# A retention-attention and MLP kernel: attention in pairs of units grouped by array tiling, far parts a period later, row factors in the masks

## The chip, the cores and the metric

The kernel runs on one core of a Trainium2 chip. The metric is the device time of one execution in microseconds. Before the change the median of 3 runs is 662.73 (660.90 to 663.81).

## What is computed

Batch 4, 8 heads, 576 positions, 64 columns per head, all in fp32 inputs. Attention without a softmax, with a decay per head, and then two MLP blocks:

```python
scores = scale * np.matmul(q, k.transpose(0, 1, 3, 2))
gamma = 1.0 - 2.0 ** (-5.0 - np.arange(H, dtype=np.float32))
Dmat = np.where(rel >= 0, gamma[:, None, None] ** rel[None, :, :], 0.0)
ret = scores * Dmat[None, :, :, :]
return np.matmul(ret, v)
...
h = gelu(x @ w_in)
u, v = (h[..., :d_ff // 2], h[..., d_ff // 2:])
v_s = np.einsum('ts,bsd->btd', w_sg, layer_norm(v) * g_ln) + b_sg[None, :, None]
x = x + (u * v_s) @ w_out
...
x = x + np.maximum((layer_norm(x) * g_ln2) @ w_ch1, 0.0) @ w_ch2
```

## The kernel before

The change lies in the first of three stages, the attention. Its work is 16 units: a unit is one batch and one pair of heads, whose 2x64 columns lie on the two halves of the 128 partitions. A sequence of 576 is four chunks of 128 and a rest of 64. Since the decay is a power of the distance, a unit needs only four products on TensorE (PE). A pair of units here is an even unit and the odd one after it; the rests of both are done together.

- `scores(n)` (L246): k times q of each chunk, two heads, into two PSUM banks. The scores are multiplied by a triangular mask with the factors of the key's row (L256): three of four masks of a pair on VectorE (DVE), the fourth copied by ScalarE (ACT, L254) and multiplied by GpSimd (POOL). For odd units also the rest scores of both units (L269, masked by L273).
- `states(n)` (L282): k, scaled by ACT beforehand (L237 in `prep_unit`), times v, per chunk; a scan on DVE (L290) adds them up with the decay into y.
- `attend_near(n)` (L315): masked scores times v.
- `attend(n)` (L327): the far part, y of the chunk before times q, added in the same bank; DVE multiplies the result by the row factors of the query (L333) on its way to SBUF. Odd units add the rest: `attend_rest` (L303, v times masked rest scores), L346 (y times q) and DVE's L350.

The array is used in parts. Scores multiply 64 rows into 128 outputs, states and near parts 128 rows into 64 outputs, far and rest parts 64 rows into 64 outputs; the two heads use two parts of the array. Each fp32 product counts as two records in the trace, so that a unit's 8 score instructions are 16 records.

The order of every engine's work is written out by hand (`manual_schedule`): instructions stand on each engine in the order of the program text, and semaphores are put where data need them. The loop over the units does at step n: the load of unit n+3 (one DMA on SP's queue, 1120 KB in a ring of five tiles), `prep_unit(n+2)`, `scores(n+1)`, a number of background steps, then the rest, `states(n+1)`, `attend_near(n)` and `attend(n)`, and more background steps. The first product of the MLP, `v_products(0, 0)`, is placed inside the last unit.

The background (`background_steps`) is a generator. It decodes weights that come as 64-bit words into fp32 and splits each into a high and a low part. A piece of 512 columns is one DMA of 512 KB (`f64_words`, L147) and four DVE instructions (L156, L160, L163, L165), one Square on ACT (L162), then a cast on ACT (L360) and a subtraction on POOL (L361), spread over four steps: w_in first (8 pieces), then w_sg (5 loads of fp32, split without a decode), then w_out and pieces of w_ch, which go back to DRAM. `UNIT` gives the number of steps at the two places of each unit; the last `LATE` pieces of w_ch are decoded in the MLP.

Before the loop, DVE forms the masks from a table (L499, L507), ACT forms the scan's decay (L524), PE makes `WARM` products of zeros (L530, two passes each) and `form_rows` makes the query's row factors with four products and an ACT copy (L515, L519). DVE, ACT, POOL and SP stand beside PE; there are eight PSUM banks, one of them for the decode.

Of the kernel before, what the change touches and what calls it, by code (L numbers as in the profile page):

```python
# [21 lines left out]
NP = H // 2  # L22
# [14 lines left out]
WARM = 3  # L37
# [9 lines left out]
LATE = 5  # L47
UNIT = "00 00 21 22 31 11 10 12 21 13 22 11 32 20 01 32".split()
# [26 lines left out]
O_MASKR = 16  # L75
O_HEAD = O_MASKR + NP * R
O_GROW = O_HEAD + C
TA = O_GROW + NP * C
TS = (NP + 1) * C
# [8 lines left out]
def const_tables():  # L88
    g = np.array(GAMMA, np.float64)
    p = np.arange(128)  # L90
    tab = np.zeros((128, TF + TS), np.float64)
# [3 lines left out]
    for hp in range(NP):  # L95
        gp = g[2 * hp + p // D][:, None]
        tab[:, O_GC + hp * NC:O_GC + (hp + 1) * NC] = gp ** C * (np.arange(NC)[None, :] > 0)
        tab[:, O_GR + hp:O_GR + hp + 1] = gp ** -(p % R)[:, None]
        tab[0:H, TF + (hp + 1) * C:TF + (hp + 2) * C] = np.arange(H)[:, None] == 2 * hp + p[None, :] // D
    tab[0:H, TF:TF + C] = g[:, None] ** np.arange(C)[None, :] / np.sqrt(D)  # L100
    return tab.astype(np.float32)
# [3 lines left out]
def kernel(  # L105
# [7 lines left out]
    tab_in: bass.AP,  # L113
    params: bass.AP,
# [74 lines left out]
    ld = es_a.enter_context(tc.tile_pool(name="ld", bufs=5))  # L189
# [8 lines left out]
    first = pa.tile([128, D * NC], F32, tag="y", bufs=3, name="first")  # L198

    def load_tab(part):  # L200
        if part == 0:
            nc.sync.dma_start(out=first[:, 0:TF], in_=tab_in[:, 0:TF])
        else:
            nc.sync.dma_start(out=tab[0:H, O_HEAD:], in_=tab_in[0:H, TF:])

    NU = B * NP
    units = {}
# [3 lines left out]
    def load_unit(n):  # L211
        t = ld.tile([128, AW], F32, tag="ld", name="ld")
        if n == 0:

            to, src = (z[:, 0:2 * S].rearrange("p (a s) -> p a s", a=2) for z in (t, attn[n]))
            for x, y in ((0, 2 * C), (2 * C, S)):
                nc.sync.dma_start(out=to[:, :, x:y], in_=src[:, :, x:y])
                if x == 0:
                    load_tab(0)
            nc.sync.dma_start(out=t[:, 2 * S:], in_=attn[n, :, 2 * S:])  # L220
        else:
            nc.sync.dma_start(out=t, in_=attn[n])
        units[n] = dict(ld=t)

    def prep_unit(n):
        u = units[n]
        hp = n % NP
        t = u["ld"]
        u["qT"] = t[:, 0:S]
        u["kT"] = t[:, S:2 * S]  # L230
        u["k"] = t[:, 2 * S:2 * S + NC * C].rearrange("p (c e) -> p c e", c=NC)
        o = 2 * S + NC * C
        v = t[:, o:]
        u["v"] = v
        for h in range(2):
            k = u["k"][:, :, h * D:(h + 1) * D]
            act.activation(out=k, in_=k, func=ACTF.Copy, scale=col(tab, 2 * hp + h))  # L237

    def scores(n):
        u = units[n]  # L240
        hp = n % NP
        p = u["p"] = pa.tile([128, 2, NC, C], F32, tag="p", name="p")
        sc = [bank() for h in range(2)]
        for c in range(NC):
            for h in range(2):
                pe.matmul(  # L246
                    sc[h][:, c * C:(c + 1) * C], u["kT"][h * D:(h + 1) * D, c * C:(c + 1) * C],
                    u["qT"][h * D:(h + 1) * D, c * C:(c + 1) * C], start=True, stop=True,
                )
        for h in range(2):  # L250
            x = sc[h].rearrange("p (c i) -> p c i", c=NC)
            on = dve
# [6 lines left out]
            free(sc[h])  # L259
        if n % 2 == 0:  # L260
            return

        rest = u["rest"] = bank()
        pr = u["pr"] = pa.tile([128, 2 * R], F32, tag="pr", name="pr")
        for x in range(2):
            w = units[n - 1 + x]
            for h in range(2):
                r = slice(h * D, (h + 1) * D)
                pe.matmul(  # L269
                    rest[r, x * R:(x + 1) * R], w["kT"][r, NC * C:], w["qT"][r, NC * C:], start=True, stop=True,  # L270
                    skip_group_check=True,
                )
        dve.tensor_tensor(out=pr, in0=rest[:, 0:2 * R], in1=col(tab, O_MASKR + (hp - 1) * R, 2 * R), op=ALU.mult)  # L273

    def states(n):
        u = units[n]
        us = bank()
        us_c = us[:, 0:NC * D].rearrange("p (e c) -> p c e", c=NC)
        for c in range(NC):
            for h in range(2):  # L280
                r = slice(h * D, (h + 1) * D)
                pe.matmul(  # L282
                    us_c[r, c], u["k"][:, c, r],
                    u["v"][:, c * C + h * D:c * C + (h + 1) * D], start=True, stop=True,
                )


        y = pa.tile([128, D * NC], F32, tag="y", bufs=3, name="y")
        u["y"] = y.rearrange("p (e c) -> p c e", c=NC)
        dve.tensor_tensor_scan(  # L290
# [1203 lines left out]
```

## Time and profile before

| | us |
|---|---|
| median of 3 runs | 662.73 |
| profiled execution | 661.1 |
| its span, first to last instruction | 659.3 |
| PE busy | 652.3 (99%) |
| DVE busy | 458.7 (70%) |
| ACT busy | 310.7 (47%) |
| POOL busy | 306.0 (46%) |
| second `v_products` starts on PE, after the attention | 78.45 |

Times inside the kernel count from the first instruction. The attention stage lies between 7.34 us, the first scores, and 78.45. A busy PE is not a PE at its peak, since matmuls are pipelined and a record overlaps the next one; so lengths are read from start to start. Waits are named by the engine that waits, then the one that ended the wait.

### The profile page before, as it was taken

How to read it: one execution, taken by the hardware profiler on the slowest of the kernel's cores; microseconds unless marked ns; L12 is line 12 of the kernel's file. 1: busy time of each engine (PE TensorE's matmuls, PEld its weight loads, DVE VectorE, ACT ScalarE, POOL GpSimd, SP SyncE). 2: the span in 40 equal slices, each digit the busy share in tenths (PEclk: the TensorE clock that was granted, in tenths of full speed). 3: DMA queues.
4: the chain of work that ended last, by engine and by line, in shares of the span. 5: the costliest groups of instructions: out<-in, count | busy, mean ns of one | idle time of the engine just before them, and what ended most of it. 6: DMA issues, size and time to landing. Idle time of an engine off the chain costs nothing.

```text
span 659.3 us, 12482 instructions
## 1 busy us (share of the span) xinstructions
PE 652.3 (99%) x4428; PEld 592.9 (90%) x4428; DVE 458.7 (70%) x925; ACT 310.7 (47%) x638; POOL 306.0 (46%) x290
## 2 busy tenths in 40 slices
PE   8999999999999999999999999999999999999997
PEld 6888899899889989998898889988898889999996
DVE  5799769789799885877888643555543345458894
ACT  4454595275277457524454533233535313335443
POOL 0354658225325617955555694265558742410000
PEclk9999999999999999999999999999999999999999
DMA  8999638677687685579996868799999689999734
GB/s 317 365 371 352 192 106 231 228 243 231 225 296 230 194 244 135 173 276 398 310 309 245 266 209 269 241 369 371 341 354 373 200 299 342 363 364 413 263 129 160
DMA packets 97230, 181.23 MB, mean 275 GB/s; under 512 B 9608, under 2 KB 47112, under 8 KB 93456
## 3 DMA queue, kind: packets, MB, share of 16 engines
q1 hardware_dynamic: 97168, 180.44, 80.7%
q8 instruction: 35, 0.57, 0.3%
q14 instruction: 27, 0.22, 0.1%
HBM read 122.99 MB, written 56.62 MB: 272 GB/s over the span
## 4 chain that ended last, share of the span: by engine, by line
PE 92%; DVE 3%; DMA 2%; ACT 2%; POOL 1%; issue 1%; SPq 0%; DVEq 0%; POOLq 0%; ACTq 0%
PE b L139 24%; PE b L137 23%; PE b L138 23%; PE b L788 6%; PE b L1265 3%; PE b L246 2%; PE b L315 2%; PE b L327 2%; PE b L1266 2%; DMA raw<-in_w_in_dram 1%; PE b L282 1%; PE b L530 1%; PE b L722 1%; PE b L721 1%; POOL vnl L645 1%
## 5 line engine op out<-in xcount | busy, mean ns | idle before, releaser
L137 PE MATMUL b<-fe,w 128*128 128x384 f32 x336 | 113.2, 337 | 0.0
L139 PE MATMUL b<-fe,w 128*128 128x384 f32 x336 | 113.0, 336 | 0.0
L138 PE MATMUL b<-fe,w 128*128 128x384 f32 x336 | 112.7, 335 | 0.0
L139 PE MATMUL b<-w,h 128*128 128x512 f32 (+1 forms) x270 | 98.1, 363 | 0.0
L138 PE MATMUL b<-w,h 128*128 128x512 f32 (+1 forms) x270 | 97.9, 363 | 0.0
L137 PE MATMUL b<-w,h 128*128 128x512 f32 (+1 forms) x270 | 96.8, 358 | 0.0
L869 POOL TENSOR_TENSOR w<-raw_w,w 128x512 fp32r<-128x512 f32 x30 | 39.6, 1321 | 58.3 <-ACT w L868 53.2
L137 PEld LDWEIGHTS b<-fe,w 128*128 128x128 f32 x336 | 63.1, 188 | 3.8 <-DVE t L1122 0.9
L138 PEld LDWEIGHTS b<-fe,w 128*128 128x128 f32 x336 | 63.1, 188 | 2.7
L139 PEld LDWEIGHTS b<-fe,w 128*128 128x128 f32 x336 | 63.0, 188 | 0.0
L139 PEld LDWEIGHTS b<-w,h 128*128 128x128 f32 x270 | 51.0, 189 | 7.7
L137 PEld LDWEIGHTS b<-w,h 128*128 128x128 f32 x270 | 51.0, 189 | 6.0 <-issue 0.2
L138 PEld LDWEIGHTS b<-w,h 128*128 128x128 f32 x270 | 50.9, 189 | 6.1
L162 ACT ACTIVATE raw<-raw 128x512 f32<-128x512 f32 x44 | 29.9, 679 | 54.5 <-DVE b L160 47.3
L1099 ACT ACTIVATE h<-b 128x384 fp32r<-128x384 f32 x32 | 15.7, 491 | 82.7 <-DVE b L1128 54.7
L589 POOL TENSOR_TENSOR st<-st,par 128x1 f32<-128x1 f32 x36 | 22.1, 616 | 49.6 <-DVE st L588 49.5
L1100 DVE SCALAR_TENSOR_TENSOR h<-b,h 128x384 fp32r<-128x384 f32 x32 | 17.8, 556 | 30.7 <-ACT h L1099 30.7
L137 PE MATMUL b<-w_sg,vnh 128*128 128x288 f32 x128 | 37.8, 295 | 0.0
L139 PE MATMUL b<-xt_hi,w_in 128*128 128x288 f32 x128 | 37.7, 295 | 0.0
L139 PE MATMUL b<-w_sg,vnl 128*128 128x288 f32 x128 | 37.7, 295 | 0.0
L138 PE MATMUL b<-w_sg,vnh 128*128 128x288 f32 x128 | 37.7, 295 | 0.0
L138 PE MATMUL b<-xt_lo,w_in 128*128 128x288 f32 x128 | 37.7, 294 | 0.0
(196 smaller groups left out, 1695.3 us busy)
## 6 DMA issues: line engine op xcount, KB each, us to landing
w<-ws_dram SPq DMA_DIRECT2D x96, 256.0 KB, 5.0
ld<-in_attn_dram SPq DMA_DIRECT2D x15, 1120.0 KB, 8.4
raw<-in_w_ch_dram SPq DMA_DIRECT2D x32, 512.0 KB, 4.9
ws_dram<-w SPq DMA_DIRECT2D x16, 896.0 KB, 7.6
w<-wb_dram SPq DMA_DIRECT2D x14, 1024.0 KB, 7.9
w_dram<-c SPq DMA_DIRECT2D x32, 256.0 KB, 3.1
wb_dram<-fe SPq DMA_DIRECT2D x32, 256.0 KB, 5.1
raw_w<-w_dram SPq DMA_DIRECT2D x30, 256.0 KB, 4.3
```

The costliest lines, as they stand in the source:

```text
L137: pe.matmul(ps, lh, rh, start=first, stop=False, skip_group_check=True)
L138: pe.matmul(ps, lh, rl, start=False, stop=False, skip_group_check=True)
L139: pe.matmul(ps, ll, rh, start=False, stop=last, skip_group_check=True)
L162: act.activation(out=f(w1), in_=f(w1), func=ACTF.Square)
L246: pe.matmul(sc[h][:, c * C:(c + 1) * C], u["kT"][h * D:(h + 1) * D, c * C:(c + 1) * C], u["qT"][h * D:(h + 1) * D, c * C:(c + 1) * C], sta ...
L315: pe.matmul(o[r, c * C:(c + 1) * C], v[:, c * C + h * D:c * C + (h + 1) * D], p[:, h, c], start=(c == 0), stop=(c == NC - 1), skip_group_c ...
L589: pool.tensor_tensor(out=st[:, 4:5], in0=st[:, 3:4], in1=col(par, O_MH), op=ALU.pow)
L788: pe.matmul(ps, g, wo[k][:, w], start=done[0] == 1, stop=done[0] == 3 * KE, skip_group_check=True)
L869: pool.tensor_tensor(out=t[:, 1], in0=raw, in1=f(t[:, 0]), op=ALU.subtract)
L1099: act.activation(out=t[:, 0], in_=v, func=ACTF.Relu)
L1100: dve.scalar_tensor_tensor(out=t[:, 1], in0=v, scalar=0.0, in1=f(t[:, 0]), op0=ALU.max, op1=ALU.subtract)
L1265: pe.matmul(ps, e[:, 0, x], t, start=begin, stop=False, skip_group_check=True)
```

## The change

The loop runs over eight pairs. In one step it does the scores and masks of both units, then the rest scores, then `finish` of the pair before (both far parts, both rest parts, and the copies to SBUF, now on ACT), then the states of both, the scans, and the near parts of both. Pairs 0 and 1 have orders of their own. A unit comes by two DMAs, kT and k in one tile (ring of 4), qT, v and the rest's v in another (ring of 6). Four units are loaded at the start, two more at the end of each step. The row factors of the query are folded into the masks (for the near part) and are multiplied onto q by POOL (for the far part), so that the results are copied without a factor. To form them, a row of 1024 numbers is spread over the partitions by products with a row of ones. w_in is loaded with the second half of its columns first. The pace of the background is now a number of steps per pair (`PAIR`), `LATE` is 6 and `WARM` is 2, and `v_products(0, 0)` follows the last `finish`.

```diff
-WARM = 3
+WARM = 2
-LATE = 5
-UNIT = "00 00 21 22 31 11 10 12 21 13 22 11 32 20 01 32".split()
+LATE = 6
+PAIR = "03 22 22 22 22 23 33 54".split()
...
     def load_unit(n):
-        t = ld.tile([128, AW], F32, tag="ld", name="ld")
+        kk = ld.tile([128, S + NC * C], F32, tag="kk", bufs=4, name="kk")
+        qv = ld.tile([128, S + NC * C + D], F32, tag="qv", bufs=6, name="qv")
...
-            nc.sync.dma_start(out=t, in_=attn[n])
+            nc.sync.dma_start(out=kk, in_=attn[n, :, 0:w])
+            nc.sync.dma_start(out=qv, in_=attn[n, :, w:])
...
+    def scale_q(n):
+        q = units[n]["qT"]
+        row = col(tab, O_LATE + n % NP * C, C)
+        x = q[:, 0:NC * C].rearrange("p (c i) -> p c i", c=NC)
+        pool.tensor_tensor(out=x, in0=x, in1=row.unsqueeze(1).to_broadcast([128, NC, C]), op=ALU.mult)
+        x = q[:, NC * C:]
+        pool.tensor_tensor(out=x, in0=x, in1=row[:, 0:R], op=ALU.mult)
...
-            if h and n % 2:
-                act.copy(p[:, h], x)
-                x, on = p[:, h], pool
-            on.tensor_tensor(
-                out=p[:, h], in0=x, in1=mask[:, 2 * hp + h].unsqueeze(1).to_broadcast([128, NC, C]), op=ALU.mult,
+            dve.tensor_tensor(
+                out=p[:, h], in0=u["sc"][h].rearrange("p (c i) -> p c i", c=NC),
+                in1=mask[:, 2 * (n % NP) + h].unsqueeze(1).to_broadcast([128, NC, C]), op=ALU.mult,
...
-        dve.tensor_tensor(
-            out=xb[b][:, hp, 0:NC * C].rearrange("p (c i) -> p c i", c=NC),
-            in0=o.rearrange("p (c i) -> p c i", c=NC),
-            in1=col(tab, O_GROW + hp * C, C).unsqueeze(1).to_broadcast([128, NC, C]), op=ALU.mult,
-        )
+        act.copy(xb[b][:, hp, 0:NC * C], u["o"])
...
+    each = [bank() for _ in range(2)]
+    for x in range(2):
+        pe.matmul(each[x], one[0:1, 0:128], grow[0:1, x * 512:(x + 1) * 512], start=True, stop=True)
...
+    def form_masks(x):
+        for h in range(x * 4, x * 4 + 4):
+            dve.scalar_tensor_tensor(
+                out=mask[:, h], in0=each[x][:, h % 4 * C:(h % 4 + 1) * C], scalar=col(first, O_GP + h),
+                in1=col(first, O_TRI, C), op0=ALU.mult, op1=ALU.mult,
+            )
...
+    def form_rows():
+        late = bank()
+        for h in range(2):
+            pe.matmul(
+                late[half[h]], one[0:1, 0:D], grow[0:1].rearrange("p (a h i) -> p a h i", h=2, i=C)[:, :, h],
+                start=True, stop=True, skip_group_check=True,
+            )
+        act.copy(col(tab, O_LATE, NP * C), late)
...
+    def finish(k):
+        for n in (2 * k, 2 * k + 1):
+            far(n)
+            put(n)
+        attend_rest(k)
+        put_rest(k)
+
+    for k in range(NPAIR):
+        a, b = 2 * k, 2 * k + 1
+        if k == 0:
+            form_masks(0)
+            scores(a)
+            form_rows()
+            masks(a)
+            scale_k(a)
+            form_masks(1)
+            form_rest()
+            states(a)
+            near(a)
+            background(1)
+            scores(b)
+            scores_rest(k)
+            masks(b)
+            scale_k(b)
+        else:
+            scores(a)
+            masks(a)
+            scale_k(a)
+            if k == 1:
+                finish(k - 1)
+            scores(b)
+            masks(b)
+            scale_k(b)
+            scores_rest(k)
+        mask_rest(k)
+        scale_q(a)
+        scale_q(b)
+        background(int(PAIR[k][0]))
+        if k > 1:
+            finish(k - 1)
+        if k:
+            states(a)
+        states(b)
+        scans(k)
+        if k:
+            near(a)
+        near(b)
+        load_unit(a + 4)
+        load_unit(b + 4)
+        background(int(PAIR[k][1]))
...
+    finish(NPAIR - 1)
```

**Where instructions moved.** PE in one pair of units before. b_76 and the like are PSUM banks; ld is a unit's loaded tile; x8 after a row is a number of equal instructions; of the eight score rows of a unit one or two stand here.

```order
L246 MATMUL b_82<-ld 128x128
L269 MATMUL b_76<-ld 64x64 x4
L282 MATMUL b_77<-ld 64x64 x8
L315 MATMUL b_78<-p,ld 64x128 x8
L327 MATMUL b_78<-ld,y 64x128 x6
L246 MATMUL b_81<-ld 128x128
...
L303 MATMUL b_76<-pr,ld 64x64 x4
L282 MATMUL b_80<-ld 64x64 x8
L315 MATMUL b_82<-p,ld 64x128 x8
L327 MATMUL b_82<-ld,y 64x128 x6
L346 MATMUL b_76<-ld,y 64x64 x4
```

PE after, from the states of pair 1 to the near parts of pair 2:

```order
L285 MATMUL b_77<-qv,kk 64x64 x16
...
L245 MATMUL b_82<-qv,kk 128x128
L245 MATMUL b_77<-qv,kk 128x128
L264 MATMUL b_79<-qv,kk 64x64 x4
L316 MATMUL b_76<-qv,y 64x128 x6
L316 MATMUL b_80<-qv,y 64x128 x6
L331 MATMUL b_78<-pr,qv 64x64 x4
L331 MATMUL b_78<-qv,y 64x64 x4
L285 MATMUL b_81<-qv,kk 64x64 x16
L307 MATMUL b_82<-p,qv 64x128 x8
L307 MATMUL b_77<-p,qv 64x128 x8
```

Groups of one kind of both units now stand together, and the far parts (L316) are those of the pair before. The scores of unit 5 use the bank b_77 in which the states of pair 1 were.

DVE after, from the last decode step of the first w_in piece (L163) to the first mask of unit 4 (L154 is the first decode step of the next piece, L295 the scans of pair 1):

```order
L163 SCALAR_TENSOR_TENSOR c<-raw,b_75 128x512 [waits DVE_49,Activation_49]
L154 TENSOR_SCALAR b_75<-raw 128x512 [waits DMAHW1_49,DVE_49]
L295 SCALAR_TENSOR_TENSOR y<-formed,b_77 128x256 [waits PE_49]
L295 SCALAR_TENSOR_TENSOR y<-formed,b_77 128x256
L158 SCALAR_TENSOR_TENSOR b_75<-raw,b_75 128x512 [waits DVE_49]
L161 SCALAR_TENSOR_TENSOR b_75<-raw,b_75 128x512 [waits DVE_49]
L251 TENSOR_TENSOR p<-b_79,formed 128x512 [waits PE_49,Activation_49]
```

Both scans of one pair and all four masks of the next now stand behind a step that waits for a load; before, one scan and the masks of one unit stood there.

ACT in the opening before (L519 is the copy of the row factors, L237 the scaling of k):

```order
L524 COPY formed<-first 128x256 x4
L237 ACTIVATE ld<-ld,tab 128x4x64 [waits DMAHW3_49,Activation_49]
L237 ACTIVATE ld<-ld,tab 128x4x64
L519 COPY tab<-b_79 128x512 [waits DMAHW4_49,PE_49]
L237 ACTIVATE ld<-ld,tab 128x4x64 [waits DMAHW5_49]
```

and after (L520 and L227):

```order
L500 COPY formed<-first 128x256 x4
L520 COPY tab<-b_81 128x512 [waits PE_49]
L227 ACTIVATE kk<-kk,tab 128x4x64 [waits DMAHW4_49,Activation_49]
L227 ACTIVATE kk<-kk,tab 128x4x64
L227 ACTIVATE kk<-kk,tab 128x4x64 [waits DMAHW6_49]
```

The copy, which waits for PE, has moved ahead of the scaling of unit 0's k.

## Rows read from the trace of the kernel before

**Rows 1.** The page, engines and costliest groups: busy us (share) xinstructions; busy, mean ns | idle

```profile
PE 652.3 (99%) x4428; PEld 592.9 (90%) x4428; DVE 458.7 (70%) x925; ACT 310.7 (47%) x638; POOL 306.0 (46%) x290
...
L869 POOL TENSOR_TENSOR w<-raw_w,w 128x512 fp32r<-128x512 f32 x30 | 39.6, 1321 | 58.3 <-ACT w L868 53.2
```

**Rows 2.** Stretches: length, busy us of PE PEld DVE ACT POOL, clock, DMA share, GB/s

```profile
20.00:60.00 40.00, 39.83 (x701) 35.22 (x696) 37.97 (x69) 21.49 (x44) 20.13 (x16) 1.00 0.97 362
30.00:40.00 10.00, 9.82 (x164) 8.52 (x164) 9.93 (x19) 6.23 (x13) 4.26 (x4) 1.00 1.01 402
60.00:70.00 10.00, 9.96 (x166) 8.64 (x164) 9.31 (x18) 5.91 (x11) 5.36 (x5) 1.00 0.74 274
90.00:100.00 10.00, 10.00 (x78) 10.00 (x77) 6.86 (x23) 9.81 (x22) 6.05 (x7) 1.00 0.29 79
```

**Rows 3.** PE's timeline over one pair: start us, us, engine, line, output, xrecords

```profile
43.82 1.16 PE L246 MATMUL b<-ld 64*128 64x128 f32 x16
44.91 0.45 PE L269 MATMUL b<-ld 64*64 64x64 f32 x8
45.29 0.69 PE L282 MATMUL b<-ld 128*64 128x64 f32 x16
45.81 1.05 PE L315 MATMUL b<-p,ld 128*64 128x128 f32 x16
46.78 0.98 PE L327 MATMUL b<-ld,y 64*64 64x128 f32 x12
47.70 1.16 PE L246 MATMUL b<-ld 64*128 64x128 f32 x16
...
50.66 0.98 PE L327 MATMUL b<-ld,y 64*64 64x128 f32 x12
51.48 0.59 PE L346 MATMUL b<-ld,y 64*64 64x64 f32 x8
52.00 0.38 PE L246 MATMUL b<-ld 64*128 64x128 f32 x2
```

**Rows 4.** PE's timeline, the opening

```profile
2.27 5.14 PE L530 MATMUL b<-zero 128*128 128x512 f32 x6 [2.27 <-ACT zero L495]
7.34 1.16 PE L246 MATMUL b<-ld 64*128 64x128 f32 x16
...
17.24 0.99 PE L327 MATMUL b<-ld,y 64*64 64x128 f32 x12
```

**Rows 5.** PE's timeline, the end of the stage

```profile
72.76 0.50 PE L137 MATMUL b<-w_in,xt_hi 128*128 128x512 f32 x1
...
75.71 0.45 PE L303 MATMUL b<-pr,ld 64*64 64x64 f32 x8
...
78.45 0.50 PE L137 MATMUL b<-w_in,xt_hi 128*128 128x512 f32 x1
```

**Rows 6.** ACT's timeline, the opening

```profile
7.70 0.91 ACT L237 ACTIVATE ld<-ld,tab 128x256 f32<-128x256 f32 x2 [2.46 <-DMA ld<-in_attn_dram]
9.62 0.59 ACT L519 COPY tab<-b 128x512 f32<-128x512 f32 x1 [1.02 <-PE b L515]
```

**Rows 7.** DVE's timeline around its wait for the second w_in piece

```profile
27.13 0.69 DVE L156 TENSOR_SCALAR b<-raw 128x512 uint32<-128x512 uint32 x1 [1.47 <-DMA raw<-in_w_in_dram]
27.73 0.68 DVE L290 TENSOR_TENSOR_SCAN y<-formed,b 128x256 f32<-128x256 f32 x1
...
28.91 0.28 DVE L350 TENSOR_TENSOR xb<-b,tab 128x128 f32<-128x128 f32 x1
29.11 0.69 DVE L160 SCALAR_TENSOR_TENSOR b<-raw,b 128x512 uint32<-128x512 uint32 x1
```

**Rows 8.** DMA issues from 4.7 to 5.0 us: KB each, us to landing

```profile
raw<-in_w_in_dram SPq DMA_DIRECT2D x1, 512.0 KB, 13.5
```

**Rows 9.** ACT's timeline, after the stage

```profile
79.21 1.28 ACT L619 ACT_TABLE_LOAD   x1
```

More of the change, by code (lines that the diff above doesn't have):

```diff
@@ L196 @@
     decay = formed[:, H * C:].rearrange("p (x n) -> p x n", x=NP)
[L198 to L204, printed above, removed]
+    first = pa.tile([128, D * NC], F32, tag="y", bufs=4, name="first")
     NU = B * NP
+    NPAIR = NU // 2
     units = {}
@@ new lines, with scores_rest, mask_rest @@
+    rests = {}
+    def scores_rest(k):
+        t = rests[k] = bank()
+        for x in range(2):
+            u = units[2 * k + x]
+            for r in half:
+                pe.matmul(
+                    t[r, x * R:(x + 1) * R], u["kT"][r, NC * C:], u["qT"][r, NC * C:], start=True, stop=True,
+                    skip_group_check=True,
+                )
+    def mask_rest(k):
+        pr = units[2 * k]["pr"] = pa.tile([128, 2 * R], F32, tag="pr", name="pr")
+        dve.tensor_tensor(
+            out=pr, in0=rests[k][:, 0:2 * R], in1=col(tab, O_MASKR + 2 * k % NP * R, 2 * R), op=ALU.mult
+        )
@@ L244, in scores, with states @@
+    sums = {}
+    def states(n):
+        k, x = divmod(n, 2)
+        if x == 0:
+            sums[k] = bank()
+        u = units[n]
+        o = sums[k][:, x * NC * D:(x + 1) * NC * D].rearrange("p (e c) -> p c e", c=NC)
         for c in range(NC):
@@ L275, in states @@
[L275 to L290, printed above, removed]
-            out=y, data0=decay[:, n % NP], data1=us[:, 0:NC * D], initial=0.0, op0=ALU.mult, op1=ALU.add
-        )
-        free(us)
@@ new lines, in states, with scans @@
+                    start=True, stop=True, skip_group_check=True,
+                )
+    def scans(k):
+        us = sums.pop(k)
+        for x in range(2):
+            y = pa.tile([128, D * NC], F32, tag="y", bufs=4, name="y")
+            units[2 * k + x]["y"] = y.rearrange("p (e c) -> p c e", c=NC)
+            dve.tensor_tensor_scan(
+                out=y, data0=decay[:, (2 * k + x) % NP], data1=us[:, x * NC * D:(x + 1) * NC * D], initial=0.0,
+                op0=ALU.mult, op1=ALU.add,
+            )
+        free(us)
@@ new lines, in attend_rest @@
+    def attend_rest(k):
+        for part in range(2):
+            for x in range(2):
+                u = units[2 * k + x]
+                for r in half:
+                    o = rests[k][r, (2 + x) * R:(3 + x) * R]
+                    if part == 0:
+                        w, z = u["v"][r, NC * C:], units[2 * k]["pr"][r, x * R:(x + 1) * R]
+                    else:
+                        w, z = u["y"][r, NC - 1], u["qT"][r, NC * C:]
+                    pe.matmul(o, w, z, start=part == x == 0, stop=part == 1, skip_group_check=True)
@@ L354, in attend, with put_rest @@
-        free(rest)
+        act.copy(xb[b][:, hp, 0:NC * C], u["o"])
+        free(u["o"])
+    def put_rest(k):
+        b, hp = divmod(2 * k, NP)
+        t = rests.pop(k)
+        act.copy(xb[b][:, hp:hp + 2, NC * C:], t[:, 2 * R:4 * R].rearrange("p (x i) -> p x i", x=2))
+        free(t)
+        for x in range(2):
+            del units[2 * k + x]
     wi, wsl, wo = [], [], []
@@ new lines, in form_rows, with form_rest @@
+    def form_rows():
+        late = bank()
+        for h in range(2):
+            pe.matmul(
+                late[half[h]], one[0:1, 0:D], grow[0:1].rearrange("p (a h i) -> p a h i", h=2, i=C)[:, :, h],
+                start=True, stop=True, skip_group_check=True,
+            )
+        act.copy(col(tab, O_LATE, NP * C), late)
+        free(late)
+    def form_rest():
+        for hp in range(NP):
+            for x in range(2):
+                r = half[x]
+                dve.scalar_tensor_tensor(
+                    out=tab[r, O_MASKR + hp * R:O_MASKR + (hp + 1) * R],
+                    in0=tab[r, O_LATE + hp * C:O_LATE + hp * C + R], scalar=first[r, O_GR + hp:O_GR + hp + 1],
+                    in1=first[r, O_TRI + x * R:O_TRI + (x + 1) * R], op0=ALU.mult, op1=ALU.mult,
+                )
```

230 lines of the change are left out of this document (71 added, 159 removed).

## The prediction, made before the changed kernel ran

> **What bounds the kernel now.** I read the page's engine lines first. PE is busy for 99% of the span and DVE for 70% [rows 1], so the end is set by PE's row of work, and an edit counts only where it shortens that row or makes PE wait. The change touches the first 78 us. There the stretches [rows 2] show what stands close behind PE: from 30 to 40 us DVE is busy for 9.93 of 10 us, and over 20 to 60 us the DMA engines are busy for 0.97 of the time at 362 GB/s. From 90 to 100 us ACT is busy for 9.81 of 10. Then I read PE's timeline over one pair of units [rows 3]: it runs from 43.82 to 52.00, 8.18 us, group after group without a wait. The opening [rows 4] and the end of the stage [rows 5] come last.
>
> **What a change of group costs PE.** Of one unit, the states (L282, 8 steps of 64 columns) take 45.81-45.29 = 0.52 us and the near part (L315, 8 steps of 128) takes 46.78-45.81 = 0.97 [rows 3]. The difference, 0.45, is 8x64 columns: 0.056 us per 64, 0.112 per 128 columns. (Two records that start together, on two parts of the array, are one step.) So pure streaming is 0.90 for the scores of a unit, 0.45 states, 0.90 near, 0.675 far (6x0.112), and 0.225 for each of three rest groups of a pair: 2x2.925+0.675 = 6.525 us. The pair takes 8.18, so 1.65 lies at the group boundaries. Read per group: scores 1.09-0.90 = 0.19, states with near 1.49-1.35 = 0.14, a lone rest group 0.38-0.225 = 0.155, a lone far group 0.92-0.675 = 0.245, and far with the L346 rest 52.00-50.66 = 1.34 against 0.90, so 0.44.
>
> **Pair by pair after the change.** A steady pair is three blocks: scores of both units 16x0.112+0.19 = 1.98; one block of the 64x64 groups (rest scores, both far parts, both rest parts), 12x0.112+12x0.056 = 2.02, with the largest boundary cost of such a block, 0.44, 2.46; states and near parts of both 2.70+0.14 = 2.84. Sum **7.3**, 0.88 less than 8.18. If each of the three boundaries costs the mean of before (1.65/8 = 0.2), it is 7.15; if nothing is saved it is 8.18. Pair 1 has its far block between the two scores: 1.09+2.24+1.09+0.38+2.84 = 7.65. The last far block, alone, is 1.35+0.45+0.44 = 2.24, and the first v product, moved behind it, takes 75.71-72.76 = 2.95 in both kernels [rows 5].
>
> **The opening gets longer.** Before, far(1) starts at 17.24 [rows 4]; by then PE has also done scores(2), states(2), far(0) and the rest group L303 (1.09+0.52+0.92+0.38), so what the new order does up to near(1) is worth 14.33. After: six warm passes take 5.14 us, 0.857 each [rows 4]; now there are four, and four passes of the two one-row products that spread the row factors. Steady 512 columns take 4x0.112 = 0.45. If six passes run at 0.857 and two at 0.45, the first score starts at 8.3 instead of 7.34. The ends are 7.4 (one-row passes at half price) and 9.1 (all at 0.857). Scores end at 9.4, the second row product (4 passes, two side by side, 0.9) at 10.3. On ACT the copy of that product now stands ahead of the two k scalings of unit 0, which before were done at 7.70 to 8.61, ahead of the copy [rows 6]: 0.1+0.55+0.91 makes states(0) start at 11.85, a wait of 1.5. Near(0) ends 13.3, scores(1) 14.4, rest scores 14.8, states(1) 15.3; near(1) needs two masks of 0.60 each on DVE [rows 7] behind scores(1), so it starts at about 15.8 and ends at **16.85**. That is 2.5 more than 14.33.
>
> **Plain sum.** 16.85+7.65+6x7.3+2.24+2.95 = 73.5, where before PE starts the second v product at 78.45 [rows 5]: -4.95.
>
> **Waits that the new order adds.** DVE runs in order, and a decode step of the background stands ahead of scans and masks. (i) The first w_in piece comes behind four units in both kernels; it was issued at about 4.9 and took 13.5 us [rows 8], so it lands at 18.4. Two DVE steps (1.2) and the Square on ACT (0.6) follow, 20.2, then scale_k(2) 0.91, the puts of pair 0 (1.2, as ACT's 128x512 copy), scale_k(3) 0.91: 23.2. PE is at states(3) at 16.85+1.09+2.24+1.09+0.38+0.45 = 22.1: +1.1, less what the masks' own order gives back, 1.0. (ii) The second piece follows two more units (1,146,880 bytes each) and its own 524,288 at 402 GB/s [rows 2]: 18.4+2x2.85+1.3 = 25.4. The first decode step (L154) waits for it ahead of the two scans of pair 1, and those free the bank into which scores(5) write: 25.4+0.6+1.2 = 27.2, while PE is there at 16.85+7.65+1.0+1.0 = 26.5. Take 1.0; ends 0 and 2.5 (the piece as late as before, where L156 waited 1.47 and started at 27.13 [rows 7]). (iii) In pairs 6 and 7 the background runs six and nine steps, and the last w_in piece comes behind units 14 and 15. The nearest row is the same wait of 1.47: take 1.5, ends 0 and 3.0. (iv) 0.3 for short waits of near parts. Together **+3.8**, and the stage ends at 77.3, 1.1 earlier.
>
> **Work moved between engines.** The row factors go into the masks and q: 16 row multiplies and 8 small ones leave DVE (0.60 and 0.20 each by its neighbours [rows 7]), four masks a pair run on DVE instead of three, and ACT copies the results out instead of copying scores. DVE's pair is then, with four decode steps, 4x0.60+0.20+2x0.60+4x0.60 = 6.2, under 7.3; with six it is 7.4. POOL multiplies q once per unit; a 128x512 operation there takes about 1.3 us by the L869 row (39.6 us for 30 [rows 1]), and a pair of 7.3 us holds two of them and its one or two other operations; far, the first reader of the chunks, comes a period later. The two DMAs per unit instead of one add 8x2 issues on SP and no bytes. Because v_products moves behind the last far block, PE has no filler there, and the last puts on ACT stand behind three w_sg copies that wait for loads.
> The Trainium skill, page "TensorEngine Tiling (Array Packing)", Performance Considerations, PSUM Bottleneck, says that packing the array speeds up TensorE but not the emptying of PSUM, which may become the bound. By that rule the gain of 0.88 a pair would not all be kept; the full DVE in the stretch from 30 to 40 us agrees with it, the sum of 6.2 does not.
>
> **Behind the stage.** Before, the table load at 79.21 [rows 9] precedes the first gelu, and ACT is then full until 100 us [rows 2], so a later first gelu reaches PE. The puts behind the w_sg copies, the sixth late w_ch piece (one more decode, 4 steps of 0.60 on DVE and one Square on ACT inside the first MLP block) and the short cover there I price at **+1.5**; ends 0 (all hidden) and 3.0 (two ACT waits like the 1.47).
>
> **Sum:** -1.1+1.5 = +0.4 against the profiled execution's 661.1 (span 659.3), whose time is 1.6 below the median of the runs, 662.73. On the median: **663.1 us**, no change. What a measurement can tell from no change here is about 0.5%, 3.3 us.
>
> **Rivals.** *A, the waits stay hidden (faster).* If pieces land a little sooner and ACT's chain has slack, neither the 3.8 nor the 1.5 reaches PE: -4.95, **657.8**. For it: PE waits almost nowhere before although DVE is full. Against: the order puts L154 straight ahead of scans and masks.
> *B, the transfers become the bound (slower).* A steady pair needs 2x1.147+0.524 = 2.82 MB. At 402 GB/s [rows 2] that is 7.0 us, hidden; at the 362 of 20 to 60 us it is 7.8, 0.5 over 7.3. It decides below 385 GB/s. Six pairs: +3.0 on the forecast, **666.1**. For: share 0.97. Against: 60 to 70 us is at 274 GB/s, so loads run ahead.
> The Trainium skill, page "DMA: Bandwidth & Descriptors", overview table, gives about 358 GB/s from HBM per core; estimated from it, a pair's transfers take 7.9 us and the result is 3.6 above the forecast. The stretch of 402 GB/s disagrees with it as a ceiling.
> *C, the boundary cost is not what grouping removes (slower).* If PE pays per step and not per change of tile form, pairs stay at 8.18 and the opening and waits are paid on top: +0.88x6 = 5.3, **668.4**. Against: two neighbours of one form (far, then rest) start 51.48-50.66 = 0.82 apart, 0.10 less than far followed by scores.
> *D, emptying PSUM binds.* DVE before is busy 8.1 of 8.18 us in a pair; less 2x0.60+0.20 and plus 0.60 that is 7.3, no slack left. With pairs at 7.6: +1.8, **664.9**. The page on array packing above names this case.
>
> **How the numbers follow.** Forecast 0.58, A 0.17, B 0.11, C 0.06, D 0.08. The range goes from A (657.8, a little widened: 657.5) to the late end of the opening, of wait (ii) and of the stage's tail together (+0.8+1.5+1.5 on the forecast, 666.9); C and the far tails, 0.13 or so, lie outside. Faster by over 0.5%: A and a sliver, 0.18. Slower: C, half of B and the forecast's upper end, 0.17. Same: 0.65.
>
> **What would show it.** Right: a steady pair of about 7.3 us on PE, the first scores near 8.3, states(0) waiting for ACT, DVE idle at L154 for the second piece, the second v product at 77 to 78. Wrong: pairs of 8 us (C), PE waits that name DMAs in every pair (B), a stage end before 75 (A).

## The result, and the profile after

| | before | after |
|---|---|---|
| median, us | 662.07 (4 runs) | 670.68 (669.97 to 673.55, 4 runs) |
| ratio, 95% interval | | 1.0136 (1.0097 to 1.0175) |
| profiled execution, its span | 661.1, 659.3 | 673.55, 671.8 |
| second v product starts on PE | 78.45 | 86.05 |
| from there to the end of the span | 580.9 | 585.8 |

The change costs 8.6 us, and the time lies above the predicted range of 657.5 to 666.9. The profiled execution is the slowest of the four. In it the attention stage ends 7.6 us later instead of 1.1 earlier, and 4.9 us more are lost behind it.

PE's timeline of the changed kernel, as [rows 4], up to the first scores of pair 1:

```profile
2.27 3.78 PE L493 MATMUL b<-zero 128*128 128x512 f32 x4 [2.27 <-ACT zero L489]
5.98 3.78 PE L497 MATMUL b<-grow,one 1*128 1x512 f32 x4
9.69 2.08 PE L245 MATMUL b<-qv,kk 64*128 64x128 f32 x16
11.70 1.97 PE L516 MATMUL b<-grow,one 1*64 1x512 f32 x4
14.76 1.41 PE L285 MATMUL b<-qv,kk 128*64 128x64 f32 x15 [1.09 <-ACT kk L227]
...
17.91 2.08 PE L245 MATMUL b<-qv,kk 64*128 64x128 f32 x16
19.92 0.69 PE L264 MATMUL b<-qv,kk 64*64 64x64 f32 x8
20.54 0.69 PE L285 MATMUL b<-qv,kk 128*64 128x64 f32 x16
...
22.38 1.16 PE L245 MATMUL b<-qv,kk 64*128 64x128 f32 x16
```

The scores of a unit take 2.01 us from start to start (9.69 to 11.70, and again 17.91 to 19.92), and 1.09 from 22.38 on; the states at 20.54 already take 0.51, as in [rows 3]. So until about 20 us PE runs at half rate, the lower of its two levels, 1.2 GHz instead of 2.4. Pair 1 starts at 22.38 where 16.85 was forecast.

Pair 2, and pair 3, the first undisturbed one, as [rows 3]:

```profile
30.11 1.38 PE L245 MATMUL b<-qv,kk 64*128 64x128 f32 x18
32.68 1.16 PE L245 MATMUL b<-qv,kk 64*128 64x128 f32 x14 [1.20 <-DVE y L295]
34.59 0.69 PE L264 MATMUL b<-qv,kk 64*64 64x64 f32 x8 [0.76 <-DVE p L251]
35.08 2.72 PE L316 MATMUL b<-qv,y 64*64 64x128 f32 x24
...
41.26 2.06 PE L245 MATMUL b<-qv,kk 64*128 64x128 f32 x32
43.26 0.45 PE L264 MATMUL b<-qv,kk 64*64 64x64 f32 x8
43.55 1.66 PE L316 MATMUL b<-qv,y 64*64 64x128 f32 x24
45.03 0.40 PE L331 MATMUL b<-pr,qv 64*64 64x64 f32 x8
45.26 0.64 PE L331 MATMUL b<-qv,y 64*64 64x64 f32 x8
45.83 1.15 PE L285 MATMUL b<-qv,kk 128*64 128x64 f32 x32
46.81 1.92 PE L307 MATMUL b<-p,qv 128*64 128x128 f32 x32
48.66 2.06 PE L245 MATMUL b<-qv,kk 64*128 64x128 f32 x32
```

Pair 3 takes 48.66-41.26 = 7.40 us (so do pairs 4 and 5) against 8.18: the grouping gains 0.78 a pair. Pair 2 takes 11.15. It waits for the scans and for a mask, and then its far block (L316 to L331) takes 2.55 instead of 1.48: most of it at half rate again. What the scans wait for is in DVE's timeline, as [rows 7]:

```profile
30.77 0.69 DVE L154 TENSOR_SCALAR b<-raw 128x512 uint32<-128x512 uint32 x1 [1.69 <-DMA raw<-in_w_in_dram]
31.37 1.25 DVE L295 TENSOR_TENSOR_SCAN y<-formed,b 128x256 f32<-128x256 f32 x2
```

and in the chain of waits is when that piece was issued: SP's queue stands at the loads of units 4 and 5 until their kk tiles are free, the first of them once PE is at the rest scores of pair 0 (L264, 19.92), and the piece is issued behind them.

```profile
20.49 0.33 SPq L217
20.86 0.63 SPq L218
21.59 0.36 SPq L217
22.00 0.43 SPq L218
22.48 8.19 DMA raw<-in_w_in_dram
```

In the kernel before the queue stands at a unit's load as well, and its second piece goes out at 18.86:

```profile
5.30 13.52 SPq L222 DMA_DIRECT2D ld<-in_attn_dram  x2
18.86 0.43 SPq L147 DMA_DIRECT2D raw<-in_w_in_dram  x1
```

Pair 7 and the end of the stage, as [rows 5], where PE waits for masks behind the last piece:

```profile
71.67 2.06 PE L245 MATMUL b<-qv,kk 64*128 64x128 f32 x32
75.49 0.45 PE L264 MATMUL b<-qv,kk 64*64 64x64 f32 x8 [1.76 <-DVE p L251]
...
86.05 0.39 PE L135 MATMUL b<-w_in,xt_hi 128*128 128x512 f32 x1
```

Stretches of the changed kernel, as [rows 2]; the columns are length, busy us of PE, PEld, DVE, ACT, POOL, granted clock, DMA share, GB/s. The clock reads 1.00 from 10 to 20 us although PE is at half rate there, so its rate is read from the products:

```profile
10.00:20.00 10.00, 8.91 (x70) 6.34 (x70) 5.68 (x14) 2.19 (x5) 1.27 (x1) 1.00 0.62 252
30.00:40.00 10.00, 8.04 (x128) 7.49 (x126) 7.39 (x13) 4.23 (x9) 4.77 (x6) 0.83 0.78 315
340.00:400.00 60.00, 56.78 (x277) 49.35 (x276) 42.93 (x70) 27.98 (x49) 36.18 (x29) 1.00 0.83 271
```

From 340 to 400 us PE is idle for 3.2 us, where it had no idle time before. PE's waits there:

```profile
PE b L135 <- DVE t L1144: 2.6, 2, 1.5
PE b L135 <- ACT u L1140: 0.6, 1, 0.6
```

### The profile page after: what moved, and what is told of

The parts are those of the page before. It is cut to its first block, busy times and chain, and to the rows that moved or that the text cites. A ratio compares the mean times of both kernels' runs of the same rounds, so it can differ in the third digit from the quotient of the medians.

```text
span 671.8 us, 12556 instructions
## 1 busy us (share of the span) xinstructions
PE 655.8 (98%) x4426; PEld 595.1 (89%) x4426; DVE 455.0 (68%) x910; ACT 315.7 (47%) x654; POOL 321.5 (48%) x314
## 4 chain that ended last, share of the span: by engine, by line
PE 75%; DMA 7%; DVE 7%; ACT 5%; issue 3%; POOL 2%; SPq 1%; ACTq 0%; DVEq 0%; POOLq 0%
PE b L137 18%; PE b L136 18%; PE b L135 18%; PE b L810 6%; PE b L1287 3%; DMA x<-z_dram 2%; PE b L245 2%; PE b L1288 2%; DMA row<-y_dram 1%; PE b L316 1%; DMA raw<-in_w_in_dram 1%; PE b L307 1%; PE b L285 1%; DVE c L163 1%; POOL vnl L667 1%
## 5 line engine op out<-in xcount | busy, mean ns | idle before, releaser
L1122 DVE SCALAR_TENSOR_TENSOR h<-b,h 128x384 fp32r<-128x384 f32 x32 | 17.8, 556 | 30.7 <-ACT h L1121 30.7
```

What stands on the lines that cost most here:

```text
L1122: dve.scalar_tensor_tensor(out=t[:, 1], in0=v, scalar=0.0, in1=f(t[:, 0]), op0=ALU.max, op1=ALU.subtract)
```

## The experiments

All but e16, an edit of the kernel before, and e17, no edit, are edits of the changed kernel. "Stage" is the start of the second v product in the profiled execution, "rest" the span from there on (78.45 and 580.9 in the kernel before). The kernel before had medians of 661.8 to 662.9 in these jobs. Measured together were e1 to e4, e5 to e8, e9 and e10, e11 to e13, e14 and e15, and e16 and e17. The unaltered changed kernel had 670.68 in its first job and 674.50 in e17's, so a difference of up to about 4 us between rows of different jobs shows nothing. The rest, too, differs from one profile to the next: it is 583.9 to 590.4 in the eight profiles of kernels with the changed kernel's own order behind the stage (the first, e1 to e4, e11, e13, e17).

| run | median, us | ratio, 95% | stage | rest |
|---|---|---|---|---|
| e1_warm3 | 670.61 | 1.0122 (1.0088-1.0156) | 84.51 | 587.4 |
| e2_rows128 | 667.12 | 1.0079 (1.0048-1.0110) | 81.05 | 584.5 |
| e3_lead2 | 670.28 | 1.0133 (1.0076-1.0189) | 81.65 | 584.5 |
| e4_opening_lead | 669.90 | 1.0119 (1.0078-1.0160) | 80.49 | 590.4 |
| e5_late5 | 672.66 | 1.0164 (1.0124-1.0204) | 80.03 | 588.8 |
| e6_rows_late5 | 670.66 | 1.0133 (1.0113-1.0152) | 79.33 | 587.9 |
| e7_opening_order | 671.98 | 1.0153 (1.0136-1.0171) | 81.49 | 588.5 |
| e8_puts_early | 671.45 | 1.0142 (1.0122-1.0162) | 81.23 | 589.5 |
| e9_all | 676.54 | 1.0193 (1.0150-1.0236) | 86.67 | 589.3 |
| e10_pace | 679.72 | 1.0254 (1.0210-1.0299) | 89.91 | 588.6 |
| e13_slots_alone | 678.04 | 1.0218 (1.0171-1.0264) | 87.17 | 583.9 |
| e11_slots | 673.64 | 1.0163 (1.0141-1.0186) | 83.20 | 584.5 |
| e12_slots5 | 671.18 | 1.0126 (1.0097-1.0156) | 79.90 | 591.0 |
| e14_late5_first | 669.77 | 1.0115 (1.0093-1.0137) | 80.22 | 586.9 |
| e15_first_order | 667.57 | 1.0077 (1.0054-1.0100) | 80.96 | 586.4 |
| e16_before_late6 | 665.73 | 1.0047 (1.0031-1.0064) | 78.51 | 585.3 |
| e17_again | 674.50 | 1.0168 (1.0141-1.0195) | 85.10 | 588.4 |

### The opening's rate: e1, e2, e17

```diff
 e1_warm3
-WARM = 2
+WARM = 3
 e2_rows128
+    dve.memset(grow, 0.0)
-        pe.matmul(each[x], one[0:1, 0:128], grow[0:1, x * 512:(x + 1) * 512], start=True, stop=True)
+        pe.matmul(each[x], one[:, 0:128], grow[:, x * 512:(x + 1) * 512], start=True, stop=True)
```

In e2 L516 is changed alike, and the row's load stands behind the table's. e17 is the changed kernel, unaltered.

> The changed kernel with WARM back at 3 (six warm passes instead of four). Rate theory: in the kernel before, the six warm passes took 5.14 us, that is five of about 0.93 and one of about 0.47, and every product after them ran at the higher rate. In the changed kernel four warm passes and four one-row passes (L497) took 0.93 each, and the scores, near parts and row products went on at half rate until 22.4 us. If the four warm passes were one too few and a one-row pass keeps a rate once it is reached, L497 now takes 0.47 a pass, the first scores start at about 9.3 and near(1) ends at about 18: 4 us faster than the changed kernel. If one-row products do not hold the rate, L497 starts at 0.47 a pass, but scores and rows fall back to half rate, near(1) ends at 22 to 23 and the time is within 1 us of the changed kernel.

> The changed kernel with the spreading products on all 128 rows: the row of factors lies in a tile of zeros and is multiplied with 128x128 ones, so L497 and L516 contract 128 rows instead of 1, with the same passes and columns and the same results; four warm passes stay. Theory that the one-row products hold PE at its lower rate: the rate now doubles after about five passes as in the kernel before, the first scores start at about 8.3 instead of 9.69 and take 1.1 instead of 2.0, near(1) ends at 17.0 to 17.8 instead of 22.4, and the time falls by 4.5 to 5.5 us. Rival, that the rate is held down by something else (the number of passes alone, or the wait for ACT at 13.7): L497 and the scores take what they took, near(1) ends at 22 to 23, time within 1 us.

> The changed kernel once more, unaltered, for a second profile of its opening. Of the five profiles with one-row products so far, two kept PE at half rate from the start to about 22 us, and three had the higher rate from about 7 us, lost it between 9 and 17 us, and had it back. If that is a matter of the execution and not of the kernel, this profile is of either kind, the second v product starts at 80 to 86, and the median is within 1.5 us of 670.7.

PE's timeline of e2 (its lines are one higher):

```profile
5.84 1.91 PE L498 MATMUL b<-grow,one 128*128 128x512 f32 x4
7.69 1.16 PE L246 MATMUL b<-qv,kk 64*128 64x128 f32 x16
8.78 1.08 PE L517 MATMUL b<-grow,one 128*64 128x512 f32 x4
10.95 1.01 PE L286 MATMUL b<-qv,kk 128*64 128x64 f32 x15 [1.09 <-ACT kk L228]
...
16.41 1.16 PE L246 MATMUL b<-qv,kk 64*128 64x128 f32 x16
```

and the stretch from 10 to 20 us, of e2 and then of e17:

```profile
10.00:20.00 10.00, 8.81 (x146) 7.72 (x148) 8.35 (x21) 2.50 (x6) 4.40 (x5) 1.00 1.01 408
```

```profile
10.00:20.00 10.00, 8.75 (x106) 7.16 (x104) 7.83 (x20) 2.19 (x5) 3.11 (x4) 0.68 0.80 300
```

With all 128 rows in use pair 1 starts at 16.41, near the forecast 16.85, and the clock stays up although PE has the same wait of 1.09 for ACT. With one-row products it falls: in e17, as in e1, e3, e5 and e13, the higher rate is reached at 6 to 7 us, granted clocks of 0.66 to 0.68 follow from 10 to 20, and pair 1 starts at 19 to 20. The first profile and e10's have no higher rate before about 20 and 18 us. Of the ten profiles with 128-row products nine read 1.00 from 10 to 20 us; e4's reads 0.84, behind a wait of 2.35. So two more warm passes (e1) do not help, and the number of rows does: pair 1 starts 2.7 us earlier in e2 than in e17 and 6.0 earlier than in the first profile, and the median is 3.5 us lower than that of e1, measured beside it. The expected 4.5 to 5.5 was that of the unluckier opening.
The Trainium skill, page "TensorE: Matmul & The Clock Gate", Part 1, says that the number of slow matmuls at a kernel's start varies from run to run. The two kinds of opening agree; that one-row products fail to hold the rate is what e2 shows.

### Loads: e3, e4

```diff
 e3_lead2
-        yield from f64_pieces(load_w_in(), 1)
+        yield from f64_pieces(load_w_in(), 2)
```

e4 adds e2's edit and moves `scale_k(a)` ahead of `form_rows()`.

> The changed kernel with two w_in pieces loaded at the first background step instead of one, so that each piece stands on the queue of SP one piece earlier, ahead of the loads of units 4 and 5, which wait for kk tiles. Theory that the held queue makes the piece late: the second piece lands at about 19 us instead of 30.7, DVE's L154 no longer waits for it, pair 2 on PE falls from 11.15 us to 7.4 to 8.0, and the wait of 1.76 in pair 7 behind the last piece goes too: 4 to 5.5 us faster than the changed kernel. Rival, that transfers as such bind: the loads of units 4 to 7 come 1.3 us later, scores wait for them, and the gain is under 1.5 us.

> The changed kernel with both edits, 128-row spreading products and two pieces ahead, and with the scaling of unit 0's k on ACT ahead of the copy of the row factors. If the opening and the late pieces are independent and together the whole loss, near(1) ends at about 16.5, the pairs take 7.4 each, and the time is 9 to 11 us under the changed kernel, 660 to 662, about that of the kernel before. If the loss lies elsewhere (the stage after it), 666 or more.

The second piece is there in time and the wait of 1.20 for the scans is gone, but 0.76 at L264 stays and waits for units' loads come in its place (in e3 0.72 and 0.78 for qv, and 1.58 for ACT's scaling). The median does not move. In e4 near(1) waits 2.35 for a mask: the eight 64x64 operations of `form_rest` take 3.85 us on DVE and stand ahead of it. The queue's order made that one landing late; mending it alone gains nothing that can be measured.

### The sixth late piece: e16, e5, e6, e14

```diff
 e16_before_late6 (the kernel before)
-LATE = 5
-UNIT = "00 00 21 22 31 11 10 12 21 13 22 11 32 20 01 32".split()
+LATE = 6
+UNIT = "00 00 21 22 31 11 10 12 21 13 22 11 32 20 01 10".split()
 e5_late5
-    ("13446", "3140", "2211", "01021"),
+    ("13446", "3140", "2222", "11121"),
-LATE = 6
+LATE = 5
 e14_late5_first (with e2's edit)
-    ("14203", "1414", "2430", "32323"),
+    ("25314", "1414", "2430", "32323"),
-LATE = 6
+LATE = 5
```

e6 is e5 with e2's edit.

> The kernel before, with one piece of the decode moved out of the attention stage: LATE 6 instead of 5, and four background steps fewer in the last unit (10 instead of 32). Nothing else of the change is in it. Theory that this alone makes PE wait between 340 and 395 us: PE's lateness against the kernel before grows by 3.5 to 5 us there, and the time is 665.5 to 667. If the wait in the changed kernel came from the late end of the attention stage, no growth there, and the time is within 1 us of the kernel before, or less by up to 1 us, since ACT has less to do around 85 us.

> The changed kernel with LATE back at 5 and the four steps of the piece that it decodes earlier added to the pace of the first MLP's fourth batch. In the changed kernel PE waits some 3 us for DVE (L135 behind L1144, the first hidden block of the second MLP, between 360 and 395 us), which the kernel before does not. Theory that the sixth late piece on DVE makes that wait: it goes, and the time falls by 2.5 to 3.5 us, to about 667.5. Rival, that the wait comes from the attention stage ending late (what follows is shifted against the stores and loads): the wait stays, time within 1 us of 670.7.

> The 128-row spreading products (667.1 us before this) together with LATE at 5. If the two losses add up, 663.5 to 664.5; what is left over the kernel before is then the late pieces of w_in, about 2 us.

> 128-row spreading products and LATE 5, with the four steps of the piece spread over the first batch's v tiles (pace 25314 instead of 14203), so that from the end of that batch on every decode step stands where it stands in the kernel before. Theory that the sixth late piece alone makes PE's lateness grow by 3.7 to 6 us between 340 and 395 us, and that the earlier attempts lost at 250 us and at 100 us only because their extra steps met a full ACT or a c tile not yet stored: no growth there and none at 250, PE's second v product 0.7 to 2.5 later than in the kernel before, another 0.5 to 1.5 at the first gated products, and a time of 663 to 665, against 667.1 with LATE 6. Rival, that any place for these four steps costs what it saves: 667 or more.

PE's waits from 340 to 400 us in e16, where the kernel before has none:

```profile
PE b L137 <- DVE t L1122: 2.9, 2, 1.5
PE b L137 <- ACT u L1118: 0.2, 1, 0.2
```

This settles it: one more piece moved from the last unit to the second MLP costs the kernel before 585.3-580.9 = 4.4 us in the profile and 3.2 us of the median, with nothing else changed. In e5, e6 and e14 the wait is gone, as expected, but the four steps cost about as much where they were put: at about 255 us in e5 and e6 (DVE waits 5.3 and 6.4 us for a tile still being stored, PE 1.9 for ACT), at about 100 us in e14 (PE waits 2.7 us for POOL, which waits for ACT, and loses 5.3 us to the end of that batch). So e5 did not come out faster; that it was slower is not shown, since its ratio lies between those of the unaltered kernel (1.0136, 1.0168). None of the places tried for the piece outside the attention stage costs less.

### The order on DVE: e7 to e13, e15

```diff
 e7_opening_order (with e6's edits)
+            scale_k(a)
             form_rows()
             masks(a)
-            scale_k(a)
-            form_masks(1)
-            form_rest()
...
             masks(b)
+            form_masks(1)
+            form_rest()
...
+        if k == 0:
+            background(1)
         load_unit(a + 4)
         load_unit(b + 4)
-        background(int(PAIR[k][1]))
+        background(int(PAIR[k][1]) - (k == 0))
 e8_puts_early (with e7's)
+        if k == NPAIR - 1:
+            finish(k)
         background(int(PAIR[k][1]) - (k == 0))
 e10_pace
-LATE = 6
-PAIR = "03 22 22 22 22 23 33 54".split()
+LATE = 5
+PAIR = "03 22 23 23 23 33 32 08".split()
 e13_slots_alone
+PAIR = "03 40 40 40 40 50 60 54".split()
 e12_slots5
+LATE = 5
+PAIR = "03 50 50 50 50 50 50 08".split()
```

e10 also has the last `finish` earlier and two steps more at the first v tile; e9 is e10 with the opening of e2 and e7 and with `form_rest` as eight plain scalings early and one multiplication. e11 is that opening with e13's pace, e12 that opening with the pace above, e15 that opening with e14's pace and e8's order.

> The kernel of the line above with three orders changed: unit 0's k scaled before the copy of the row factors (ACT), the masks of heads 4 to 7 and the rest's masks formed after unit 1's scores are masked (DVE), and the second w_in piece put on SP's queue ahead of the loads of units 4 and 5. If waits for ACT, DVE and the held queue are what is left: near(1) ends at 14.5 to 15.5 instead of 16.4, no wait of PE for ACT at 11 us, pair 2 under 8 us, the second v product starts at about 77 to 78 and the time is 660 to 661.5. If other waits take their place, 663 or more.

> The kernel of the line above with the last finish ahead of the last background steps, so that the last results are copied by ACT before the w_sg copies that wait for loads. If the first gelu's lateness (83.6 against 80.5 before) reaches PE, another 0.5 to 1.5 us faster; if it is hidden behind the v products, no difference.

> A version against all the losses seen so far: 128-row spreading products; unit 0's k scaled ahead of the row copy; masks of heads 4 to 7 behind unit 1's; the rest's masks formed early by plain scalings (0.27 us each in the kernel before, instead of 0.48) and multiplied by the rows in one step, so that they no longer stand ahead of the scans (in the run before this, that cost a wait of 3.1 us of the far part); second w_in piece ahead of units 4 and 5; LATE 5 with its four steps in pairs 2 to 7 and at the first v tile instead of the fourth batch (where they made a wait of 1.9 us for ACT and a fall of the clock near 290 us); last results copied before w_sg. If the waits were the whole loss, near(1) ends at 15 to 16, pairs take 7.4 to 7.7, the second v product starts at 75 to 76.5 against 78.45 in the kernel before, and the time is 658 to 660, below both. If transfers bind in pairs 3 to 6, whose background is faster now, or the later stages wait again, 662 to 667.

> The changed kernel with only the pace of the line above: LATE 5, PAIR 03 22 23 23 23 33 32 08, two more steps at the first v tile, the last finish ahead of the w_sg steps. Theory that the sixth late piece makes the wait of PE for DVE between 360 and 395 us, and nothing else does: that wait is gone, the opening is as in the changed kernel, the time is 2.5 to 3.5 us less, about 667.5. Rival, that a late attention stage makes waits wherever it meets the pace: a wait of the same size stands elsewhere, time within 1 us of 670.7.

> The changed kernel with only the places of the background steps moved: PAIR 03 40 40 40 40 50 60 54, the same number of steps in each pair, but all between the rest's mask and the scans instead of half behind the scans. In the runs so far PE waits for DVE's masks at the rest scores (L264, 0.4 to 1.8 us a pair) and for the scans, because on DVE a decode step, sometimes one that waits for its load, stands ahead of both scans and four masks. Theory that DVE's order binds the later pairs: the waits of PE at L264 in pairs 2 and 7 and at L245 in pair 2 (4.3 us together) fall to under 1.5 us, and the time falls by 2 to 4 us, to 667 to 668.5. Rival, that the late loads bind wherever the steps stand: scans and masks wait for the same landing, time within 1 us of 670.7.

> The same places of the steps together with the 128-row spreading products, the rest's masks formed early, unit 0's k scaled first, the masks of heads 4 to 7 later and the second w_in piece ahead of units 4 and 5; LATE stays 6. If opening and DVE's order are the whole loss of the attention stage, pairs of 7.4 to 7.6 throughout, the second v product at 75.5 to 77, and the time 661 to 663, with the wait of about 3 us between 360 and 395 us still there. If waits take their places again, 666 or more.

> The line above with LATE 5: five steps in each of pairs 1 to 6, all ahead of the scans, eight in the last pair behind the last finish, two more at the first v tile. If five steps a pair fit beside the masks and scans (4x0.60+0.20+1.20+5x0.65 = 7.05 us of a 7.4 us pair), the time is 658 to 660, below both kernels. If DVE binds at five steps, or loads come late for them, 665 or more.

> The line above with the opening's order mended (unit 0's k scaled first, masks of heads 4 to 7 later, rest's masks formed early), the second w_in piece ahead of units 4 and 5, and the last results copied before the last w_sg pieces. If the steps ahead of the scans in the later pairs are what is left, the second v product starts within 0.7 us of the kernel before (78.45) and the time is 661 to 663: no gain over the kernel before, though each undisturbed pair takes 7.4 instead of 8.18 us. If the mended opening brings its 1 to 2 us to the end, 659 to 661.

In e7 and e8 near(1) ends at 15.9 and 15.2, but the scans now stand behind `form_rest` and the far part waits 3.1 us for them. e8's earlier copies bring nothing that stands out of the scatter. The pace decides more. PE's waits of e9 from 20 to 70 us, with five and six steps a pair in pairs 2 to 6:

```profile
PE b L265 <- DVE p L252: 5.3, 5, 1.6
PE b L246 <- DVE y L296: 2.0, 1, 2.0
```

Five waits for masks and one for scans, and the granted clock falls to 0.78 from 60 to 70 us, where two waits of 1.96 and 1.59 stand. With some of the steps ahead of the scans and some behind, a faster background thus goes with a later stage (86.67 and 89.91), although five steps would fit by DVE's sum (7.05 us in a pair of 7.4, as e12's expectation has it). It is the places that decide there: e12 differs from e9 in `PAIR` alone, with 30 steps in pairs 1 to 6 of both, all ahead of the scans, and its stage ends at 79.90, with no wait above 1.01 and the clock at 1.00 from 10 to 80 us. It then loses behind the stage (granted clock 0.74 from 100 to 120 us, rest 591.0). But moving all steps of the changed kernel ahead of the scans (e13) takes the waits at L264 away and puts 5.0 us of waits for the scans in their place; e11 likewise (3.2, with 0.8 left at L265). So the theory that the steps' places alone bind falls for the changed kernel's own pace, and so does its rival in part: with the same pieces landing, scans wait where masks did. What is left open is an order that keeps e12's stage and loses nothing behind it. The best of these, e2 and e15, are still 0.8% slower than the kernel before; no version here beats it.

## Why the prediction was wrong

**Right.** The grouping's gain: 7.40 us a pair measured, 7.3 forecast, 8.18 before, so rival C is out. Pair 1 (7.73 for 7.65) and the last far block (2.33 for 2.24) fit too. The wait of states(0) for ACT was there (1.09 for 1.5), and so were the waits behind L154. With full rate in the opening (e2) pair 1 starts at 16.41, near the forecast 16.85.

**Wrong, the opening: "If six passes run at 0.857 and two at 0.45, the first score starts at 8.3".** It starts at 9.69 in one profile and 7.94 in the other, which a range of 7.4 to 9.1 nearly covers. (The 0.857 is a mean of two rates: a pass takes 0.93 at the lower and 0.46 at the higher.) What failed is the next step, which prices the scores, rows and states after it at full rate. With the one-row products PE did not hold that rate, and pair 1 starts at 22.4 or 19.1 instead of 16.85.

**Wrong, wait (ii): "Take 1.0; ends 0 and 2.5".** Pair 2 lost 3.75. The landing was reckoned as 25.4 and came at 30.7, since SP's queue waits for a kk tile that PE, at half rate, frees late. In e2, at full rate, the piece is issued at 16.15 and DVE starts on it at 25.06, as reckoned. But in the first profile PE comes later as well, so the landing alone does not make the loss. Waits (i) and (ii) trade places: in e2 pair 1 takes 9.00, with waits of 0.24 and 0.34 for ACT at the states, and the scans are waited for by 0.19; in the first profile wait (i) does not show and the scans are waited for by 1.20. Pairs 1 and 2 together were forecast at 16.95 with both waits; they took 17.88 in e2 and 18.88 in the first profile. There, after 1.20 and 0.76 us of waits, the far block ran 1.07 us longer, mostly at half rate (granted clock 0.83 in that stretch). No term of the sum had the clock. Not every such wait has a slow stretch behind it: after 1.01 and 0.76 in e1, and 2.03 and 0.76 in e10, L316 takes 1.49; why, is open. Wait (iii) was 1.5 and measured 0.8+1.8 = 2.6 in pairs 6 and 7; in pair 6 PE waits 0.56 for ACT's xt_hi, not for a mask.

**Wrong, behind the stage: "(one more decode, 4 steps of 0.60 on DVE and one Square on ACT inside the first MLP block) and the short cover there I price at +1.5".** It measured 4.9 in the first profile and 7.5 in e17's; 4.4 of such a loss comes with the sixth late piece alone (e16). The puts and the short cover, the other terms of that price, cost 0.5 at most in the first profile: the last product of the first MLP's grem tiles (L810; L788 before) starts at 292.7 against 284.6, 8.1 later, where the stage ended 7.6 later. The other 4.4 is lost after that. The text priced the piece by its own length, in the first MLP block, and put it beside free work. In fact DVE's order from 340 to 400 us feeds PE's products for the hidden layer of the second MLP, and a piece more makes them wait, twice up to 1.5 us.

Together: +5.5 in the opening, +2.7 more in pair 2 than forecast, +1.1 in pairs 6 and 7, -1.0 for wait (i), +3.4 behind the stage, and 0.4 in small terms (each pair 0.1 longer than forecast, less the 0.3 of wait (iv)): 12.1 beside the +0.4 forecast, which makes the 12.45 by which the profiled executions differ (673.55-661.1). The median, 8.6, is less since the profiled execution was the slowest.

**The rivals.** None was the case as written. B was to decide below 385 GB/s; pairs 3 to 5 had 364 GB/s and still ran at 7.40 with no wait for a DMA, though in e17 and e3 PE does wait 2.2 and 1.5 us for units' loads. D comes nearest: masks and scans on DVE decide in pairs 2 and 7, but by their place behind decode steps, not by DVE's sum: in pairs 3 to 5 DVE is busy for 19.57 of 22.21 us. The Trainium skill's section on the PSUM bottleneck (page "TensorEngine Tiling (Array Packing)", Performance Considerations) says that emptying PSUM may become the bound. The undisturbed pairs at 7.40 do not show that, and the waits for masks in e9 follow the places of the decode steps, since e12, with as many steps, has 0.9 of them instead of 5.3.

## What to carry to other kernels

Grouping by array tiling is worth what the boundaries cost (here 0.78 of 8.18 us a pair), but it asks for all masks and scans of a pair at once, so every background step on the in-order engines has to be placed anew; look at what a step waits for, not only at how long it takes. Price moved background work where it will land, with the waits of whoever stands behind it, not by its own length. And where PE's opening has to bring up the clock, use products over all rows, and allow for a half-rate stretch behind a wait of PE of a microsecond or two: it came after some of them here, not after all.

## What was not expected of the hardware

With products over one row in the opening PE did not hold its higher rate, and with products of the same length over 128 rows it did (granted clock 0.66 to 0.68 in five profiles against 1.00 in nine of ten, from 10 to 20 us). The granted clock's column reads 1.00 in the first 20 us of the first profile although every product there ran at half rate (0.93 us for 512 columns, 0.46 in e2): the column did not show the level that the kernel began with. A 64x64 operation with two tensors and a scalar took 0.42 to 0.48 us on DVE (eight in 3.34 us in e7 and in 3.85 in e4), where a mask of 128x512, eight times as many columns, took about 0.6.
